# A causal convolution and a routed mixture of experts: a list scheduler with other priorities, and half of the experts' low parts on another engine

## The chip, the core and the metric

One core of a Trainium2 chip runs the kernel. Its engines are TensorE (PE in the profile: matrix products, with PEld for its weight loads), VectorE (DVE), ScalarE (ACT), GpSimd (POOL) and SyncE (SP), each with a queue of its own that is worked off in program order; semaphores order the engines among each other. The metric is the device time of one execution in microseconds.

## The reference

14336 tokens (4 sequences of 3584) of width 192. First a causal convolution with seven taps, whose weights are a softmax for each token and head, then a layer that sends each token to the two best of eight experts:

```python
w = softmax(weight_gen)                       # [B, S, 8 heads, 7 taps]
x = sum over k of w[..., k] * x_pad[s + k]     # causal, 24 columns a head -> N=14336, D=192
logits = x @ w_gate
noisy  = logits + log1p(exp(x @ w_noise)) * noise
top2   = two largest of 8; top2_w = softmax over the two
for e in 8 experts: out[mask] += top2_w * (relu(x[mask] @ w1[e]) @ w2[e])   # w1 192x1024, w2 1024x192
```

## The kernel before

**Chunks.** The tokens go through in 14 chunks of 1024 (8 groups of 128; the first chunk in two halves). For each, `conv` makes the softmax and the seven taps on VectorE: 13 operations on 128x1536 elements (lines 323 and 333, tiles `acc` and `tmp`). `split` writes the result as a float16 high part (ScalarE, line 344) and low part (VectorE, line 348) into a record tile `rec`, of which there are three (RBUF); the high part therefore waits for the scatters of three chunks earlier. `gate` multiplies it with the gate weights on TensorE (line 377, tile `bank`), VectorE adds that up (`lgt`, line 392), `routing` finds the two experts of each token and its place in their queues, with a prefix product on TensorE (lines 500 and 501), and `scatters` sends the records with 16 indirect DMAs of GpSimd (line 407) into the experts' queues `xg` in device memory. `scatter` puts a small memset of a tile `spacer` ahead of each (line 406).

**Rounds.** A round takes 256 rows of each expert's queue: 14 such rounds and one of 128; round c follows chunk c. `prologues` (SP) loads the rows' places and gates (line 794) and the transposed rows `xT` (line 800). Then for each expert four slices: `mm1` (line 856, ten products of 128x256 into a PSUM tile `pm`), `relus` (ScalarE's `hi`, line 871; VectorE's `lo`, line 875), `mm2` (line 896, twelve products of 128x192 into `py`), so 32 slices a round; `finish` multiplies with the gate (ScalarE's `y`, line 908) and adds into `out` with two indirect DMAs of GpSimd for each expert (line 913), a `nop` ahead of each.

**Weights.** They are wanted as float16 high and low parts that together carry a scaled float32 weight. `weights` takes sums of squares (ScalarE, line 678), makes a power of two of them, and writes the high parts (ScalarE). `lows` makes the low parts on TensorE: a float32 product of the weight with a diagonal matrix `dg` (line 715) minus the high part (line 716, `minus` is a negative unit matrix), eight tiles `sums` an expert, each read out by ScalarE (line 719). The parts of the first experts are made ahead of round 0, the others during it.

**What sets the order.** The program is made by a list scheduler, `Sched`. Every stream above is a generator that yields (engine, planned duration, emit, dependencies). The scheduler finds the stream that could start first, and among those on its engine that could start within WAIT of it, takes the one of the highest priority, the second argument of `spawn`. Some priorities are functions: `due` for weights, `hurry` for the routing, which rises when the rounds come near (NEAR, HURRY). GL, AL, ML, UL and XL are planned latencies. The planned times set the order alone; on the chip each engine waits on semaphores, in that order.

Of the kernel before, what the change touches and what calls it, by code (L numbers as in the profile page):

```python
# [41 lines left out]
NEAR = 5  # L42
HURRY = 10
# [6 lines left out]
GL, AL, ML, UL, XL = 5.0, 2.0, 5.0, 15.0, 6.0  # L50


class Sched:
# [90 lines left out]
def moe_kernel(ctx, tc, x_lay, wgen, noise, wgn, w1, w2, xg, out):  # L144
# [131 lines left out]
    def conv(c):  # L276
# [15 lines left out]
        for si in of_chunk[c]:  # L292
# [42 lines left out]
            sch.spawn(split(si, tm["acc"], ta), 12 if c == 0 else 6)  # L335

    def split(si, acc, ta):
# [21 lines left out]
        sch.spawn(gate(si), 12 if c == 0 else 7)  # L359
# [73 lines left out]
    def routing(c):  # L433
# [104 lines left out]
        sch.spawn(scatters(c, pos[0], t), 5)  # L538
        base = fs.tile([P, E], F32, name="begin")
        d = dve(8)  # L540
        for q, (cc, b) in enumerate(ROUNDS):
# [15 lines left out]
            sch.spawn(strays(q, t1), 4)  # L557
# [109 lines left out]
    def due(e):  # L667

        return 10 if e < 2 or e - at[0] < NEAR else 2

    def weights(e):
# [22 lines left out]
        dg = hp.tile([P, 2, P], F32, name="dg", bufs=2)  # L694
        for i in range(2):
            td = yield ("ACT", act(P), lambda: A.activation(dg[:, i], ident, AF.Copy, scale=q[:, 1, i:i + 1]),
                        [t] + before("low", e, 2))
# [3 lines left out]
        ts = yield (None, 0.0, None, [ta])  # L701
        sch.spawn(lows(e, dg, ((wb, u, u2, 0), (wa, t1, t2_, 0), (wc, h2, l2, 1)), td, ts), lambda: due(e))

    def lows(e, dg, parts, td, ts):

        for w, h, l, i in parts:
            n = 512 // w.shape[2]
            n = n if w.shape[1] % n == 0 else 2
            for a in range(0, w.shape[1], n):
# [403 lines left out]
```

## Time and the profile before

| | |
|---|---|
| timed runs, median of 3 | 1298.4 us (1297.04 to 1300.36) |
| the profiled execution, its own time | 1293.18 us |
| its span | 1291.4 us |
| mean granted clock of TensorE, share of full | 0.955 |

The span is what the trace covers; 1.8 us lie around it. The median of the timed runs is 5.2 us above the profiled execution's own time. The rows read from the trace stand below, in groups.

### The profile page before, as it was taken

The page shows a single profiled execution, that of the slowest core. Times are in us where ns is not written, and L with a number is a line of the kernel's source. Part 1 is how long each engine was busy: PE and PEld are TensorE (multiplying, and loading weights), DVE is VectorE, ACT ScalarE, POOL GpSimd, SP SyncE. Part 2 cuts the span into 40 slices and gives each one's busy share as a digit, 9 for nine tenths or more (in the row PEclk, how much of TensorE's full clock was granted, in tenths as well). Part 3 has the DMA queues.
Part 4 walks back from the last instruction along what each step waited for, and adds up shares of the span by engine and source line. Part 5 has one row for each costly group of instructions (what it writes and reads, how often), then busy time and mean ns, then how long its engine had stood idle before and what let it go on. Part 6 is the DMA issues. An engine that isn't in the chain of part 4 may idle for free.

```text
span 1291.4 us, 27931 instructions
## 1 busy us (share of the span) xinstructions
PE 1101.0 (85%) x10958; PEld 975.8 (76%) x10958; DVE 813.7 (63%) x1540; ACT 549.6 (43%) x1231; POOL 731.2 (57%) x781
## 2 busy tenths in 40 slices
PE   0267999999969979889869889969799999999994
PEld 0033677988968969678859879869688889999994
DVE  5447858778868878677858778858644533333331
ACT  6587774444424334324333434323323333333331
POOL 0025165475876847658466574867756777333332
PEclk9998998999999999889989999989898999999997
DMA  9952585537536475455564737546273544334331
GB/s 254 300 164 57 113 203 81 124 75 142 111 58 147 125 98 125 75 104 128 89 126 73 144 65 137 113 60 101 51 102 68 89 82 78 45 50 48 38 39 20
DMA packets 249686, 132.49 MB, mean 103 GB/s; under 512 B 182096, under 2 KB 242000, under 8 KB 247888
## 3 DMA queue, kind: packets, MB, share of 16 engines
q1 hardware_dynamic: 205392, 85.37, 30.3%
q0 software_dynamic: 44160, 45.31, 22.5%
q8 instruction: 86, 1.41, 0.5%
q14 instruction: 48, 0.39, 0.1%
HBM read 38.70 MB, written 58.10 MB: 75 GB/s over the span
## 4 chain that ended last, share of the span: by engine, by line
PE 67%; issue 7%; DMA 7%; ACT 5%; DVE 5%; POOL 4%; SPq 3%; another core or an unknown queue 1%; ACTq 0%; POOLq 0%; DVEq 0%
PE pm L856 34%; PE py L896 29%; POOL xg L407 3%; DMA out<-y,token 2%; PE sums L715 2%; ACT junk L269 2%; DMA xt<-x_lay 2%; SPq L794 1%; POOL out L913 1%; DVE acc L333 1%; DVE tmp L323 1%; DMA xg<-rec,pos 1%; SPq L370 1%; DMA xT<-xg 1%
## 5 line engine op out<-in xcount | busy, mean ns | idle before, releaser
L856 PE MATMUL pm<-xT,wres 128*128 128x256 f16 (+1 forms) x4800 | 601.9, 273 | 27.9 <-DMA xT<-xg 17.9
L913 POOL DMA_INDIRECT out<-y,token x232 | 407.6, 1757 | 364.5 <-ACT y L908 175.2
L896 PE MATMUL py<-wres,hi 128*128 128x192 f16 x3712 | 509.7, 249 | 48.7 <-ACT y L908 18.4
L875 DVE SCALAR_TENSOR_TENSOR lo<-pm,hi 128x512 f16<-128x512 f32 x464 | 316.5, 687 | 345.6 <-ACT hi L871 282.5
L856 PEld LDWEIGHTS <-wres 128*128 128x128 f16 x4800 | 455.5, 99 | 85.6 <-issue 21.5
L871 ACT ACTIVATE hi<-pm 128x512 f16<-128x512 f32 x464 | 275.5, 596 | 568.8 <-PE pm L856 454.4
L896 PE MATMUL py<-wres,lo 128*128 128x192 f16 x1856 | 461.9, 249 | 17.0 <-DVE lo L875 10.5
L896 PEld LDWEIGHTS <-hi 128*128 128x128 f16 x3712 | 343.8, 99 | 71.0 <-issue 39.9
L407 POOL DMA_INDIRECT xg<-rec,pos x224 | 281.3, 1256 | 78.8 <-issue 52.4
L896 PEld LDWEIGHTS <-lo 128*128 128x128 f16 x1856 | 183.7, 99 | 21.1 <-DVE lo L875 13.7
L333 DVE TENSOR_TENSOR acc<-acc,tmp 128x1536 f32<-128x1536 f32 (+1 forms) x90 | 147.9, 1643 | 0.9
L323 DVE TENSOR_TENSOR tmp<-xt,wt 128x1536 f32<-128x1536 f32 (+1 forms) x90 | 147.8, 1643 | 0.7
L908 ACT ACTIVATE y<-py,gate 128x192 f32<-128x192 f32 x232 | 95.5, 418 | 67.0 <-PE py L896 41.5
L406 POOL MEMSET spacer<- 1x1 f32 x224 | 63.5, 283 | 0.1
L715 PE MATMUL sums<-wres,dg 128*128 128x512 f32 (+1 forms) x96 | 53.2, 639 | 7.6 <-ACT wres L719 5.9
L269 ACT ACTIVATE junk<-xt 128x192 f16<-128x192 f32 x118 | 42.7, 362 | 21.9 <-DMA xt<-x_lay 18.6
L529 POOL TENSOR_SCALAR rec<-rr 128x8 f32<-128x8 f32 x14 | 4.5, 319 | 80.4 <-DVE rr L478 79.5
L348 DVE TENSOR_TENSOR rec<-acc,rec 128x512 f16<-128x512 f32 (+2 forms) x30 | 26.8, 898 | 31.8 <-ACT rec L344 31.1
L719 ACT ACTIVATE wres<-sums 128x512 f16<-128x512 f32 (+1 forms) x64 | 34.1, 541 | 25.7 <-PE sums L716 21.2
L715 PEld LDWEIGHTS sums<-wres,dg 128*128 128x128 f32 x96 | 18.2, 215 | 28.2 <-ACT wres L719 17.8
L377 PE MATMUL bank<-wga,xtg 128*128 128x32 f16 x224 | 15.1, 180 | 24.9 <-DMA xtg<-rec 24.5
L598 PE MATMUL sums<-ss,ones 128*128 128x2 f32 x32 | 6.9, 313 | 34.5 <-ACT junk L678 28.0
(132 smaller groups left out, 510.6 us busy)
## 6 DMA issues: line engine op xcount, KB each, us to landing
xt<-x_lay SPq DMA_DIRECT2D x13, 1344.0 KB
out<-zrec SPq DMA_DIRECT2D x14, 768.0 KB
wres<-w SPq DMA_DIRECT2D x6, 768.0 KB
out<-y,token POOLq DMA_INDIRECT x232
xg<-rec,pos POOLq DMA_INDIRECT x224
wt<-wgen SPq DMA_DIRECT2D x14, 224.0 KB
wres<-w SPq DMA_DIRECT2D x6, 512.0 KB
wres<-w SPq DMA_DIRECT2D x12, 256.0 KB
```

The lines of the kernel that those rows point to most:

```text
L269: nc.scalar.activation(q, xtile[s][:, i - first], AF.Square, accum_out=nrm[:, i:i + 1])
L323: V.tensor_mul(tm[key].rearrange("p j (h g) -> p j h g", h=H), xt[:, t:t + n].rearrange("p j (h g) -> p j h g", h=H), w[:, a:a + n].rearra ...
L333: ta = yield ("DVE", cc, lambda: V.tensor_add(tm["acc"], tm["acc"], tm["tmp"]), [])
L406: nc.gpsimd.memset(spacer, 0.0)
L407: i = nc.gpsimd.indirect_dma_start(out=xg, out_offset=bass.IndirectOffsetOnAxis(ap=idx, axis=0), in_=src, in_offset=None)
L715: nc.tensor.matmul(o, dg[:, i], w[:, a:a + n], start=True, stop=False)
L856: nc.tensor.matmul(dst, w[:, c0:c0 + 128], m, start=i == 0, stop=i == 4)
L871: nc.scalar.activation(h[0][:, :n], pm[:, :n], AF.Relu)
L875: T["lo", si] = yield ("DVE", dve(n), lambda: nc.vector.scalar_tensor_tensor(h[1][:, :n], pm[:, :n], 0.0, h[0][:, :n], op0=OP.max, op1=OP. ...
L896: nc.tensor.matmul(dst, h[:, cols], w[:, c0:c0 + D], start=begin, stop=f == F // P - 1 and i == 2, skip_group_check=True)
L908: nc.scalar.activation(y[0], o.py[t // 2][:, (t % 2) * D:(t % 2 + 1) * D], AF.Copy, scale=gate_of[o.c][:, o.e, t:t + 1])
L913: i = nc.gpsimd.indirect_dma_start(out=out, out_offset=bass.IndirectOffsetOnAxis(ap=token[o.c][:, o.e, t:t + 1], axis=0), in_=y[0], in_off ...
```

## The change

All literal priorities become a table PR with other numbers, among them 12.1 where the second chunk's convolution had 3, and 12.3 where `finish` had 7.5. NEAR, HURRY, WAIT and the planned latencies change, and so do two of the planner's durations for GpSimd (1.5 to 1.6, 1.4 to 1.85). Low parts stay on TensorE for experts 0, 4, 5 and 6 (LOWPE); for 1, 2, 3 and 7 they are three `scalar_tensor_tensor` of VectorE, of 1024, 1024 and 1536 elements a partition. The `nop` ahead of each addition becomes a memset of `spacer`, as the scatters have it.

```diff
-NEAR = 5
-HURRY = 10
+NEAR = 2
+HURRY = 12
-GL, AL, ML, UL, XL = 5.0, 2.0, 5.0, 15.0, 6.0
+LOWPE = (0, 4, 5, 6)
+WAIT = 0.29
+PR = dict(split=1.0, gate=8.7, conv1=12.1, conv=4.3, route=7.6, idle=8.7, scatter=1.8, stray=2.1, gates=5.7,
+          finish=12.3, relu=11.4, norms=4.0, rows=9.0, wload=1.0, due=12.1, undue=4.3)
+GL, AL, ML, UL, XL = 3.9, 0.9, 4.4, 17.1, 15.4
...
-            sch.spawn(convs(k + 1), 3)
+            sch.spawn(convs(k + 1), PR["conv1"] if k == 0 else PR["conv"])
...
-                t = yield ("POOL", 1.5, lambda: scatter(c, pos[:, s, i:i + 1], rec[c][:, i, :]), [t0, "zeroed"], 0.37)
+                t = yield ("POOL", 1.6, lambda: scatter(c, pos[:, s, i:i + 1], rec[c][:, i, :]), [t0, "zeroed"], 0.37)
...
+        if e not in LOWPE:
+            sch.spawn(low2(e, lambda: V.scalar_tensor_tensor(
+                l2, wc, q[:, 1, 1:2], h2, op0=OP.mult, op1=OP.subtract), tw), lambda: due(e))
...
+        if e in LOWPE:
+            sch.spawn(lows(e, dg, ((wb, u, u2, 0, 4), (wa, t1, t2_, 0, 4), (wc, h2, l2, 1, 2)), td, ta), lambda: due(e))
+        else:
+            sch.spawn(low1(e, lambda: V.scalar_tensor_tensor(
+                u2, wb, q[:, 1, 0:1], u, op0=OP.mult, op1=OP.subtract), tu,
+                lambda: V.scalar_tensor_tensor(t2_, wa, q[:, 1, 0:1], t1, op0=OP.mult, op1=OP.subtract), ta),
+                lambda: due(e))
+
+    def low1(e, fu, tu, fa, ta):
+        yield ("DVE", dve(F) + 0.06, fu, [tu])
+        T["low1", e] = yield ("DVE", dve(F) + 0.06, fa, [ta])
+
+    def low2(e, fn, t):
+        T["low2", e] = yield ("DVE", dve(8 * D) + 0.06, fn, [t])
...
-                nc.gpsimd.nop()
+                nc.gpsimd.memset(spacer, 0.0)
...
-            ta = yield ("POOL", 1.4, add, [ty + (AL if o.c else 0.0), ("clear", ROUNDS[o.c][0]), ("token", o.c)] + before("added", bi, 1), 0.27)
+            ta = yield ("POOL", 1.85, add, [ty + (AL if o.c else 0.0), ("clear", ROUNDS[o.c][0]), ("token", o.c)] + before("added", bi, 1), 0.27)
...
-                sch.spawn(finish(bj, t), 7.5)
+                sch.spawn(finish(bj, t), PR["finish"])
...
-            sch.spawn(relus(si), 8)
+            sch.spawn(relus(si), PR["relu"])
```

Of the instructions, ScalarE loses 32 read-outs of low parts and eight of the diagonals, TensorE 32 of the 64 tiles, VectorE gains 12 and GpSimd 232 memsets. The lines of the changed kernel lie some 4 to 24 further down than those before.

Where that puts the instructions is shown at three places. **The head, VectorE.** Before, chunk 0's `lgt` and routing follow on chunk 0's low parts (`rec_285`) and the beginning of chunk 1's softmax (`sm`, `wt`):

```order
L348 TENSOR_TENSOR rec_285<-acc,rec_285 128x4x128
L348 TENSOR_TENSOR rec_285<-acc,rec_285 128x4x64
L286 TENSOR_REDUCE sm<-wt 128x64
L287 TENSOR_TENSOR wt<-wt,sm 128x448
L392 TENSOR_REDUCE lgt<-bank 128x64 x2
L450 TENSOR_TENSOR lgt<-lgt,iv 128x128
L456 TENSOR_SCALAR uu<-wide 128x64
```

After, the second half of `lgt` stands behind the thirteenth and last of the 128x1536 operations of chunk 1's convolution:

```order
L327 TENSOR_TENSOR tmp<-xt,wt 128x1536
L337 TENSOR_TENSOR acc<-acc,tmp 128x1536
L396 TENSOR_REDUCE lgt<-bank 128x64
L454 TENSOR_TENSOR lgt<-lgt,iv 128x128
L691 TENSOR_TENSOR iw<-q 128x1 x2
L613 TENSOR_SCALAR q<-q 128x2 x2
L290 TENSOR_REDUCE sm<-wt 128x64
L460 TENSOR_SCALAR uu<-wide 128x64
```

The whole convolution of chunk 1 has moved from behind chunk 0's routing to ahead of it. Two of VectorE's new low parts stand inside that routing and four behind its end.

**Round 0, ScalarE.** Each read-out `wres<-sums` stands for one tile of low parts on TensorE ahead of it. Before, in the middle of round 0:

```order
L719 ACTIVATE wres<-sums 128x4x128 x2
L871 ACTIVATE hi_1110<-pm_1015 128x512
L871 ACTIVATE hi_1116<-pm_1064 128x512
L908 ACTIVATE y_1119<-py,gate 128x192
L719 ACTIVATE wres<-sums 128x2x192
L908 ACTIVATE y_1128<-py,gate 128x192
```

After, from the last read-out of all on:

```order
L743 ACTIVATE wres<-sums 128x2x192
L894 ACTIVATE hi_1144<-pm_1112 128x512
L894 ACTIVATE hi_1181<-pm_1154 128x512
L682 ACTIVATE junk,ss<-wab 128x1024
L931 ACTIVATE y_1206<-py,gate 128x192
L894 ACTIVATE hi_1226<-pm_1187 128x512
```

Of the tiles, 33 stand behind the first slice of round 0 before, and 5 after, the last of them behind its fourth slice.

**Chunks 9 and 12, GpSimd and ScalarE.** Here the numbers of the tiles are kept; chunk 9 and chunk 12 share a record buffer, `rec2`. Before, GpSimd, the last of chunk 9's scatters (`rec2_8714`):

```order
L407 DMA xg<-rec2_8714,pos_10934 131072x196
L913 DMA out<-y4_11463,token_10538 14592x192
L913 DMA out<-y5_11500,token_10538 14592x192
L406 MEMSET spacer_126 1x1
L407 DMA xg<-rec2_8714,pos_10934 131072x196
L913 DMA out<-y0_11590,token_10538 14592x192
```

and ScalarE, where chunk 12's high part (`rec2_11675`) waits for that scatter:

```order
L908 ACTIVATE y0_11590<-py_11468,gate_10537 128x192
L871 ACTIVATE hi3_11608<-pm3_11579 128x512
L908 ACTIVATE y1_11624<-py_11468,gate_10537 128x192
L871 ACTIVATE hi4_11639<-pm4_11611 128x512
L871 ACTIVATE hi2_11671<-pm2_11645 128x512
L344 ACTIVATE rec2_11675<-acc_11153 128x8x192
L871 ACTIVATE hi0_11704<-pm0_11677 128x512
```

After, GpSimd, the last of chunk 9's scatters (`rec2_9070`):

```order
L410 MEMSET spacer_126 1x1
L411 DMA xg<-rec2_9070,pos_10329 131072x196
L935 MEMSET spacer_126 1x1
L936 DMA out<-y4_11142,token_10215 14592x192
L935 MEMSET spacer_126 1x1
L936 DMA out<-y5_11189,token_10215 14592x192
```

and ScalarE, chunk 12's high part (`rec2_12245`):

```order
L894 ACTIVATE hi1_12202<-pm1_12173 128x512
L931 ACTIVATE y3_12211<-py_12037,gate_11368 128x192
L461 ACTIVATE ln_12151<-uu_12150 128x64
L894 ACTIVATE hi2_12239<-pm2_12213 128x512
L348 ACTIVATE rec2_12245<-acc_11719 128x8x192
L894 ACTIVATE hi0_12273<-pm0_12248 128x512
```

Before, the scatter stands behind the addition of `y5_11500`, and the high part that needs its buffer two `y` later on ScalarE. After, it stands ahead of the addition of `y4_11142`, and the high part behind `y3_12211`, eighteen `y` later. The last scatter of chunk c stands ahead of round c's beginning by so many additions, for chunks 1 to 7: before 11, 8, 8, 10, 6, 8, 11; after 6, 6, 6, 8, 8, 8, 10.

## Rows read from the trace of the kernel before

**Rows 1.** The page, part 1: each engine's busy time, its share of the span, and its instructions.

```profile
PE 1101.0 (85%) x10958; PEld 975.8 (76%) x10958; DVE 813.7 (63%) x1540; ACT 549.6 (43%) x1231; POOL 731.2 (57%) x781
```

**Rows 2.** Busy time by stage. Columns: the stage from and to, its length, then busy time and instructions of PE, PEld, DVE, ACT and POOL, TensorE's granted clock as a share of full, the DMA engines' busy share, GB/s. The stages are the head, round 0, rounds 1 to 11 and round 12.

```profile
0.00:123.04 123.04, 48.90 (x150) 23.11 (x151) 74.27 (x155) 87.26 (x211) 26.06 (x58) 0.97 0.73 199
123.04:232.50 109.46, 104.12 (x833) 79.20 (x833) 78.05 (x137) 69.92 (x152) 47.90 (x59) 0.95 0.64 125
232.50:1103.80 871.30, 778.81 (x8035) 711.88 (x8033) 603.77 (x1157) 328.66 (x747) 589.52 (x617) 0.95 0.54 100
1103.80:1170.50 66.70, 66.70 (x708) 63.08 (x706) 23.04 (x40) 25.04 (x49) 25.39 (x19) 1.00 0.39 49
```

**Rows 3.** What TensorE waits for in rounds 1 to 11 (232.5 to 1103.8 us): its line, what ended the wait, us in total, times, the longest.

```profile
PE py L896 <- ACT y L908: 18.4, 4, 11.5
PE py L896 <- ACT hi L871: 18.3, 3, 9.3
PE py L896 <- issue: 18.0, 29, 4.2
PE pm L856 <- DMA xT<-xg: 16.4, 3, 8.4
PE py L896 <- DVE lo L875: 10.5, 7, 4.5
PE pm L856 <- issue: 9.5, 25, 0.9
```

**Rows 4.** The timeline of the head: start, duration, engine, line, instruction, and in brackets the idle time before it and what ended it. VectorE's routing and convolution, GpSimd's first and last scatters with one memset, the first product of round 0.

```profile
69.85 0.29 DVE L392 TENSOR_REDUCE lgt<-bank 128x64 f32<-128x128 f32 x1 [14.48 <-PE bank L377]
86.09 0.17 DVE L536 TENSOR_TENSOR rec<-gg,rec 128x8 f32<-128x8 f32 x1
93.14 1.76 DVE L323 TENSOR_TENSOR acc<-xt,wt 128x1536 f32<-128x1536 f32 x1
...
87.30 1.19 POOL L407 DMA_INDIRECT xg<-rec,pos  x1 [11.19 <-DVE mask L572]
88.50 0.09 POOL L406 MEMSET spacer<- 1x1 f32 x1
88.79 0.97 POOL L407 DMA_INDIRECT xg<-rec,pos  x1 [0.20 <-issue]
90.07 0.97 POOL L407 DMA_INDIRECT xg<-rec,pos  x1 [0.23 <-issue]
99.50 1.49 POOL L407 DMA_INDIRECT xg<-rec,pos  x1 [0.22 <-issue]
112.06 1.49 POOL L407 DMA_INDIRECT xg<-rec,pos  x1 [0.22 <-issue]
...
123.04 0.38 PE L856 MATMUL pm<-xT,wres 128*128 128x256 f16 x2 [1.57 <-DMA xT<-xg]
```

**Rows 5.** The low parts on TensorE: first one tile in the timeline, its two lines; then the busy time of PE and PEld in round 0 of line 715 alone, and of line 716 alone.

```profile
128.19 1.02 PE L715 MATMUL sums<-wres,dg 128*128 128x512 f32 x2
129.05 0.38 PE L716 MATMUL sums<-wres,minus 128*128 128x512 f16 x1
...
123.04:232.50 109.46, 33.98 (x66) 11.62 (x66) 0.95 0.64 125
...
123.04:232.50 109.46, 12.31 (x33) 3.43 (x33) 0.95 0.64 125
```

**Rows 6.** Groups of VectorE instructions by line and shape, over the whole span: busy time, mean ns of one, idle time before them and what ended it. The first has two inputs in SBUF and 1024 elements a partition, the second 1536.

```profile
L348 DVE TENSOR_TENSOR rec<-acc,rec 128x1024 f16<-128x1024 f32 x13 | 15.9, 1222 | 24.9 <-ACT rec L344 24.2 <-issue 0.4 <-POOL spacer L406 0.2
L333 DVE TENSOR_TENSOR acc<-acc,tmp 128x1536 f32<-128x1536 f32 x78 | 136.4, 1749 | 0.5
```

**Rows 7.** Timeline of rounds 9 and 10, ScalarE's records and the product behind each; then the busy times, as in rows 2, of the 4.9 us behind the first.

```profile
860.18 1.48 ACT L344 ACTIVATE rec<-acc 128x1536 f16<-128x1536 f32 x1 [12.90 <-DMA xg<-rec,pos]
862.21 0.50 PE L896 MATMUL py<-wres,hi 128*128 128x192 f16 x2 [9.31 <-ACT hi L871]
931.44 1.48 ACT L344 ACTIVATE rec<-acc 128x1536 f16<-128x1536 f32 x1 [9.92 <-DMA xg<-rec,pos]
933.47 0.50 PE L896 MATMUL py<-wres,hi 128*128 128x192 f16 x2 [7.14 <-ACT hi L871]
...
862.20:867.10 4.90, 4.02 (x22) 3.00 (x23) 4.79 (x12) 2.27 (x6) 2.15 (x2) 0.50 0.62 72
```

**Rows 8.** Timeline, the first products of rounds 3 and 5.

```profile
385.81 1.03 PE L856 MATMUL pm<-xT,wres 128*128 128x256 f16 x4 [8.36 <-DMA xT<-xg]
554.34 0.82 PE L856 MATMUL pm<-xT,wres 128*128 128x256 f16 x3 [6.71 <-DMA xT<-xg]
```

**Rows 9.** Timeline of GpSimd in round 9: an addition, a memset and a scatter, and two additions on end.

```profile
847.94 1.58 POOL L913 DMA_INDIRECT out<-y,token  x1 [0.30 <-issue]
848.92 0.63 POOL L406 MEMSET spacer<- 1x1 f32 x1
849.83 0.98 POOL L407 DMA_INDIRECT xg<-rec,pos  x1 [0.27 <-issue]
853.63 1.60 POOL L913 DMA_INDIRECT out<-y,token  x1 [0.30 <-issue]
855.54 1.55 POOL L913 DMA_INDIRECT out<-y,token  x1 [0.30 <-issue]
```

More of the change, by code (lines that the diff above doesn't have):

```diff
@@ L334, in conv @@
             T["conv", si] = tn
-            sch.spawn(split(si, tm["acc"], ta), 12 if c == 0 else 6)
+            sch.spawn(split(si, tm["acc"], ta), 12 if c == 0 else PR["split"])
     def split(si, acc, ta):
@@ L358, in split @@
         T["loa", si] = yield ("DVE", dve(n * 64), lambda: lows(D, 128, 64), [t])
-        sch.spawn(gate(si), 12 if c == 0 else 7)
+        sch.spawn(gate(si), 12 if c == 0 else PR["gate"])
     def gate(si):
@@ L424, in hurry @@
     def hurry(c):
-        return 7 if upto[c] - at[0] < HURRY else 2.5
+        return PR["route"] if upto[c] - at[0] < HURRY else PR["idle"]
     def route(c):
@@ L537, in routing @@
         T["bend", c] = t
-        sch.spawn(scatters(c, pos[0], t), 5)
+        sch.spawn(scatters(c, pos[0], t), PR["scatter"])
         base = fs.tile([P, E], F32, name="begin")
@@ L556, in routing @@
             T["batch", q] = tb
-            sch.spawn(strays(q, t1), 4)
+            sch.spawn(strays(q, t1), PR["stray"])
     def strays(q, t):
@@ L667, in due @@
     def due(e):
-        return 10 if e < 2 or e - at[0] < NEAR else 2
+        return PR["due"] if e < 2 or e - at[0] < NEAR else PR["undue"]
     def weights(e):
@@ L681, in weights @@
         wc = wc.rearrange("p c d -> p (c d)")
-        for i, x in ((0, wa), (2, wb), (1, wc[:, :4 * D]), (3, wc[:, 4 * D:])):
-            t = yield ("ACT", act(x.shape[1]) + 0.19, lambda: square(i, x), [("wc" if i % 2 else "wab", e)]
+        for i, x, m in ((0, wa, F), (2, wb, F), (1, wc[:, :4 * D], 4 * D), (3, wc[:, 4 * D:], 4 * D)):
+            t = yield ("ACT", act(m) + 0.19, lambda: square(i, x), [("wc" if i % 2 else "wab", e)]
                        + before("scaled", e, 2))
@@ L693, in weights, with diagonal @@
         free = [(k, i) for i in range(e - 1) for k in ("low1", "low2")]
[L694 to L697, printed above, removed]
+        if e in LOWPE:
+            dg = []
+            def diagonal(i):
+                if not i:
+                    dg.append(hp.tile([P, 2, P], F32, name="dg", bufs=2))
+                A.activation(dg[0][:, i], ident, AF.Copy, scale=q[:, 1, i:i + 1])
+            for i in range(2):
+                td = yield ("ACT", act(P), lambda: diagonal(i), [t] + before("dg", LOWPE.index(e), 2))
@@ L704, in lows @@
+    def low1(e, fu, tu, fa, ta):
[3 more added lines that the diff above has]
+        T["low2", e] = yield ("DVE", dve(8 * D) + 0.06, fn, [t])
     def lows(e, dg, parts, td, ts):
[L706 to L709, printed above, removed]
+        for k, (w, h, l, i, n) in enumerate(parts):
+            m = n * (D if i else P)
+            for a in range(0, F // P, n):
@@ L713, in add_up @@
                     box.append(hps.tile([P, 512], F32, name="sums", bufs=2))
-                    o = box[0][:, :n * w.shape[2]]
-                    nc.tensor.matmul(o, dg[:, i], w[:, a:a + n], start=True, stop=False)
+                    o = box[0][:, :m]
+                    nc.tensor.matmul(o, dg[0][:, i], w[:, a:a + n], start=True, stop=False)
                     nc.tensor.matmul(o, minus, h[:, a:a + n], start=False, stop=True)
                 def take():
-                    nc.scalar.activation(l[:, a:a + n], box[0][:, :n * w.shape[2]].rearrange(
+                    nc.scalar.activation(l[:, a:a + n], box[0][:, :m].rearrange(
                         "p (f c) -> p f c", f=n), AF.Copy)
-                k = sums[0]
+                u = sums[0]
                 sums[0] += 1
-                m = n * w.shape[2]
-                t = yield ("PE", 5 * m / 2400 + 0.1, add_up, [td, ts] + before("sum", k, 2))
-                t = T["sum", k] = yield ("ACT", act(m), take, [t])
-            if i or w is parts[1][0]:
+                t = yield ("PE", 5 * m / 2400 + 0.1, add_up, [td, ts] + before("sum", u, 2))
+                t = T["sum", u] = yield ("ACT", act(m), take, [t])
+            if k:
                 T["low2" if i else "low1", e] = t
-        T["low", e] = t
+        T["dg", LOWPE.index(e)] = t
     outz = out[:NTOK].rearrange("(p n) d -> p n d", p=P)
@@ L982, in moe_kernel @@
     sch.spawn(n_loads(), 3)
-    sch.spawn(weight_loads(), 3.5)
-    sch.spawn(norms(), 11)
+    sch.spawn(weight_loads(), PR["wload"])
+    sch.spawn(norms(), PR["norms"])
     sch.spawn(gate_weights(), 13)
@@ L990, in moe_kernel @@
     sch.spawn(clear(), 2)
-    sch.spawn(prologues(), 6)
+    sch.spawn(prologues(), PR["rows"])
     sch.spawn(tensor(), 1)
```

7 lines of the change are left out of this document (3 added, 4 removed).

## The prediction

> **What bounds the kernel now.** I read the busy times first: TensorE works 1101 us of a span of 1291, VectorE 814, GpSimd 731, ScalarE 550 [rows 1]. The table by stage then says where TensorE isn't kept busy [rows 2]. Its first line is the head, up to the first product of round 0: 123.0 us with 48.9 of TensorE work. The second is round 0, 109.5 us. The third is rounds 1 to 11, 871.3 us, or 79.2 each, with 778.8 busy. The fourth is round 12, where TensorE is busy for all of 66.7 us. So 66.7 is the price of a round without a stall, and rounds 1 to 11 lie 871.3 − 11 × 66.7 = 138 above it. A few of the 138 are the gate and prefix products of later chunks, which round 12 no longer has; most of it is stalls and what follows them. The waits of TensorE in that stage [rows 3] have no single owner: 18.4 us for ScalarE's y, 18.3 for its hi, 18.0 and 9.5 of issue, 16.4 for the transposed rows xT, 10.5 for VectorE's lo. A stall costs twice: after the one at 862.2 the granted clock is 0.50, the lower of the two levels, for the 4.9 us that I looked at [rows 7]. So the order of each engine decides, and the order is what is changed.
>
> **The change part by part.** The sum is made against the profiled execution: span 1291.4, its own time 1293.2. The median of the timed runs is 1298.4, or 5.2 more, and I add that at the end.
>
> *The head.* The first product of round 0 waits for the rows that chunk 0's 16 scatters write [rows 4]. Before, VectorE does chunk 0's routing at once: the reduction into lgt at 69.85, after an idle time of 14.48, the last of the records at 86.09, the first scatter at 87.30, the last at 112.06 (ending 113.55), the product at 123.04. After, the 13 large operations of chunk 1's convolution stand ahead of that reduction. They are 13 × 1.75 = 22.8 us [rows 6], and some 3.3 of small softmax operations go with them; the 14.48 of idle time takes in part. So the reduction comes 22.8 + 3.3 − 14.5 = 11.6 late. Six of the new VectorE low parts also stand between there and the first scatter's mask; two of them lie inside the routing itself (1.75 + 1.22 = 3.0). I take 14.7 for both. The scatters then last 26.25 as before, and the last leg 9.5. Term: **+15**. Bounds: +6 if the idle time takes in the small operations too and the scatters, with less beside them, keep the pitch of 1.28 that the first of them have (16 × 1.28 = 20.5); +22 if all six low parts (two of 1.75 and four of 1.22, 8.4) come ahead of it and every scatter takes 1.49.
>
> That scatters beside VectorE are slower is seen in [rows 4]: 0.97 at 88.79, before the convolution starts at 93.14, and 1.49 at 99.50 and 112.06 beside it. The Trainium skill ("SBUF — State Buffer", Who interferes with whom) infers the other thing, that a tensor_tensor does not hold up descriptor generation. By it the scatters of chunk 0 would take 0.97 whatever runs beside them, 16 × 0.52 = 8 us less at most, an estimate. The measurement here differs and decides.
>
> *Round 0.* 32 of the 64 tiles of low parts leave TensorE. Of the tiles still to do once round 0 has begun, 33 stand there before and 5 after, by the order of the two programs: 28 fewer. Price of one: the groups of its two lines cover 33.98 + 12.31 = 46.3 us in round 0 [rows 5], at most 1.40 each, but matmuls overlap in the records; a tile that starts at 128.19 has its second matmul at 129.05, so 0.9 is the floor. Round 0 is 109.5 − 66.7 = 42.8 above a round without stalls, so one tile can't be worth over 42.8/33 = 1.30. I take 1.1, in the middle: 28 × 1.1 = **−31** (bounds −25 and −36). What they become costs VectorE 2 × 1.22 + 1.75 = 4.2 us an expert [rows 6], 16.8 for four; nine of the twelve instructions stand in the head, three in round 0, where VectorE has 109.5 − 78.1 = 31 us idle [rows 2]. ScalarE loses 32 read-outs, which nothing waits for any longer.
>
> *Rounds 1 to 11, ScalarE.* Twice ScalarE stands in its own order at the operation that writes the records of a chunk (rec) and waits 12.90 and 9.92 us for scatters that read the same buffer three chunks earlier; the hi behind it is late, and TensorE waits 9.31 and 7.14 [rows 7]. Before, chunk 12's rec stands two y later than the addition behind which chunk 9's last scatters stand; after, it stands 18 y later, and chunk 13's likewise. Both waits should go: 16.5, and the 4.9 and 5.4 us behind them at half the clock give back about half, 5.1. Term: **−21.5**; the bound is 0, if another instruction becomes the late one.
>
> *Rounds 1 to 11, xT.* Round 5 begins 6.71 and round 3 begins 8.36 late, for rows just scattered [rows 8]. Chunk 5's last scatter stood 6 additions ahead of the round's end, after it 8; its prefix product stands 6 slices earlier too. So the 6.71, and 2.8 for the clock behind it, go: −9.5. Chunks 2 and 3 move the other way, from 8 additions ahead to 6. At 1.9 an addition [rows 9] each may come 3.8 later, 7.6 in all; half of it is taken, since chunk 5's pitch is no rule for the others: +3.8. Chunk 1's scatters stand between more additions than before (11 ahead to 6): +3. Term: **−2.7**, bounds −20 and +11.
>
> *Rounds 1 to 11, the rest.* Issue and y [rows 3] are 46 us for which I see no reason in the order either way. The convolutions stretch from 27.4 to 29.8 slices a chunk, which thins VectorE's load; I take 0, bounds −20 and +12.
>
> *Memsets at additions.* Scatters have had one ahead of them all along: 0.97 each at a pitch of 1.27. An addition, with a nop ahead, takes 1.55, and addition follows addition at 855.54 − 853.63 = 1.91 [rows 9]. Behind the addition of 847.94 the memset starts 0.98 later and ends with it, so that the scatter starts 1.89 behind the addition. No row has a memset ahead of an addition. Nearest for no gain: 1.89 against 1.91, the tail of 0.57 stays with the addition even where a memset follows. Nearest for a gain: the same indirect DMA as a scatter has no such tail, 0.57 × 16 = 9.1 us of GpSimd a round. For a loss: the memset's 0.63, seen there, plus 0.27 of issue, 0.9. I take 0, since the two pitches agree and the memset can run ahead of what the addition waits for.
>
> The sum: 1293.2 + 15 − 31 − 21.5 − 2.7 = 1253.0, and with 5.2, **1258**.
>
> **The rivals.**
> *The memset shortens additions.* GpSimd is busy 589.5 of 871.3 in rounds 1 to 11 and runs without a pause through each chunk's scatters, so up to 9.1 a round could come off; over 11 rounds a quarter to a third of that, about 27: 1258 − 27 = 1231. For it: scatters beside memsets have no tail. Against it: 1.89 and 1.91. The order may also remove stalls of the kind that I set at 0, with a like result. Together 0.25.
>
> *The waits come back.* Rounds 1 to 11 stay at 871, because a list order freed at one place waits at the next (five kinds of wait of 10 to 18 us each stand there now [rows 3]). Then only head and round 0 count: 1293.2 + 15 − 31 + 5.2 = 1282. Chance 0.15.
>
> *The memset lengthens additions: slower.* At 0.9 each GpSimd has 14.4 us more a round, of the 79.2 − 53.6 = 25.6 that it has free. With a third of it on the path, 4.8 × 11 = 53: 1311. It decides from the point where it eats the 40 us of the sum, 40/11/16 × 3 = 0.68 us an addition. Against it: the memset waits for nothing but the memset ahead of it, and takes 0.09 between scatters, which keep their pitch with one each [rows 4]. Chance 0.08.
>
> **How the numbers follow.** My forecast, 1258, has 0.45, with a range of its own of 1238 to 1277. The gain rival has 0.25, the returning waits 0.15, the slower one 0.08; 0.07 is left for mixtures, 0.02 of it faster, 0.03 about level and 0.02 slower. What a measurement of this kernel tells from no change is about 0.3%, or 4 us: faster is below 1294.5, slower above 1302.3. The returning waits end at 1282, but 0.03 of them come close enough to count as the same. Faster 0.45 + 0.25 + 0.12 + 0.02 = 0.84, same 0.06, slower 0.10. The range leaves out the slower cases and the farthest of the gain: 1212 to 1292.
>
> **What would show it.** Right: the first product of round 0 at 131 to 145 us; round 0 near 78; no wait of ScalarE over 5 us at a rec in rounds 9 to 11; round 5 starting without a wait; additions at a pitch near 1.9. Wrong: the mean of an addition at 1.0 to 1.2 us instead of 1.76 (the gain rival); a memset of 0.6 ahead of each addition and a pitch of 2.5 (the slower one); rounds 1 to 11 still near 79 each, with TensorE's waits under other names (the waits that come back); a head past 145 us.

## The result and the profile after

The changed kernel takes 1208.0 us (median of 4; 1205.5 to 1214.4) beside 1297.7 of the kernel before: ratio 0.933, 95% interval 0.930 to 0.936. The changed kernel ran twice more beside the kernel before, with 0.945 (0.942 to 0.949) and 0.940 (0.935 to 0.945); the chips differ, so ratios to the kernel before on the same chip are compared below. The forecast was 1258 with a range of 1212 to 1292: the direction was right, the size too small, the result just below the range. One profile among those below, that of a_al14 (AL at 1.4), is of an execution 1.6% above the fastest of its kernel.

The profiled execution took 1206.6 us, its span 1204.7. Busy times, for [rows 1]:

```profile
PE 1051.8 (87%) x10862; PEld 953.8 (79%) x10862; DVE 825.7 (69%) x1552; ACT 526.0 (44%) x1191; POOL 749.8 (62%) x1013
```

The stages of [rows 2]: head, round 0, rounds 1 to 11, round 12, and the last part, whose length was 54.3 before.

```profile
0.00:140.40 140.40, 48.64 (x161) 23.37 (x162) 113.24 (x194) 99.68 (x235) 25.63 (x55) 0.74 0.75 198
140.40:217.60 77.20, 70.57 (x726) 64.02 (x726) 58.15 (x121) 37.80 (x87) 51.63 (x73) 0.98 0.60 123
217.60:1021.80 804.20, 763.60 (x8033) 704.81 (x8034) 596.08 (x1144) 324.54 (x747) 600.41 (x791) 0.98 0.59 109
1021.80:1088.40 66.60, 66.60 (x707) 62.98 (x705) 23.58 (x41) 25.41 (x49) 29.84 (x41) 1.00 0.39 53
...
1155.00:1204.70 49.70, 35.83 (x538) 35.60 (x536) 12.25 (x21) 13.65 (x26) 16.11 (x21) 0.89 0.30 29
```

So the head grew by 17.4, round 0 lost 32.3, rounds 1 to 11 lost 67.1, the last part 4.6: together −86.6. The 17.4 leans on one execution of the kernel before: b_mem, below, has the order of before and a head of 128.5, and the changed kernel's heads were 139.8 to 141.2. What TensorE waits for in rounds 1 to 11, for [rows 3]:

```profile
PE pm L879 <- DMA xT<-xg: 21.1, 4, 8.8
PE pm L879 <- issue: 6.2, 21, 0.4
PE py L919 <- issue: 5.5, 16, 0.5
PE py L919 <- ACT hi L894: 4.0, 1, 4.0
...
PE py L919 <- ACT y L931: 2.4, 1, 2.4
PE py L919 <- DVE lo L898: 1.3, 4, 0.7
```

Most of the waits for y (18.4 before), hi (18.3), lo (10.5) and issue (27.5) are gone. Those for xT are not: of the 21.1, 6.2 end with the first product of round 1 and so lie in round 0, which leaves 14.9 in the stage beside 16.4 before. Fewer stalls are also less time at the lower of the two clocks: the granted clock of the stage rose from 0.95 to 0.98, and TensorE's busy time fell from 778.8 to 763.6 for as many matmuls. So of the 67.1, 15 are the same work done in less time, and 52 are idle time that is gone (92.5 before, 40.6 after).

### The profile page after: what moved, and what is told of

It reads as the page before. It is cut to its first block, busy times and chain, and to the rows that moved or that the text cites. A ratio compares the mean times of both kernels' runs of the same rounds, so it can differ in the third digit from the quotient of the medians.

```text
span 1204.7 us, 27979 instructions
## 1 busy us (share of the span) xinstructions
PE 1051.8 (87%) x10862; PEld 953.8 (79%) x10862; DVE 825.7 (69%) x1552; ACT 526.0 (44%) x1191; POOL 749.8 (62%) x1013
## 3 DMA queue, kind: packets, MB, share of 16 engines
q1 hardware_dynamic: 205392, 85.37, 32.3%
q8 instruction: 85, 1.39, 0.5%
## 4 chain that ended last, share of the span: by engine, by line
PE 52%; POOL 15%; DMA 10%; DVE 7%; issue 6%; ACT 6%; SPq 4%; another core or an unknown queue 0%; POOLq 0%; DVEq 0%; ACTq 0%
PE pm L879 27%; PE py L919 24%; POOL xg L411 8%; POOL out L936 7%; DMA xt<-x_lay 3%; DMA out<-y,token 3%; SPq L817 2%; DVE acc L337 2%; DVE tmp L327 2%; DVE lo L898 2%; DMA xg<-rec,pos 1%; DMA xT<-xg 1%; DMA wres<-w 1%; ACT junk L682 1%; ACT junk L273 1%
## 5 line engine op out<-in xcount | busy, mean ns | idle before, releaser
L879 PE MATMUL pm<-xT,wres 128*128 128x256 f16 (+1 forms) x4800 | 594.3, 271 | 30.2 <-DMA xT<-xg 23.4
L919 PE MATMUL py<-wres,hi 128*128 128x192 f16 x3712 | 503.3, 247 | 9.8 <-ACT hi L894 4.0
L411 POOL DMA_INDIRECT xg<-rec,pos x224 | 292.0, 1304 | 76.4 <-issue 67.5
L935 POOL MEMSET spacer<- 1x1 f32 x232 | 102.8, 443 | 0.1
L410 POOL MEMSET spacer<- 1x1 f32 x224 | 53.3, 238 | 0.1
L602 PEld LDWEIGHTS sums<-ss,ones 128*128 128x128 f32 x32 | 7.1, 282 | 43.0 <-ACT junk L682 43.0
L739 PE MATMUL sums<-wres,dg 128*128 128x512 f32 (+1 forms) x48 | 29.3, 698 | 5.3 <-ACT wres L743 3.1
L739 PEld LDWEIGHTS sums<-wres,dg 128*128 128x128 f32 x48 | 9.9, 230 | 22.3 <-ACT wres L743 10.4
```

Of the source, the lines that this page charges most:

```text
L410: nc.gpsimd.memset(spacer, 0.0)
L411: i = nc.gpsimd.indirect_dma_start(out=xg, out_offset=bass.IndirectOffsetOnAxis(ap=idx, axis=0), in_=src, in_offset=None)
L879: nc.tensor.matmul(dst, w[:, c0:c0 + 128], m, start=i == 0, stop=i == 4)
L919: nc.tensor.matmul(dst, h[:, cols], w[:, c0:c0 + D], start=begin, stop=f == F // P - 1 and i == 2, skip_group_check=True)
L935: nc.gpsimd.memset(spacer, 0.0)
```

## Experiments

Each runs beside the kernel before on the same chip. "Rounds" is rounds 1 to 11 of its profiled execution, and "lag" the number of hi of later slices that stand ahead of a block's second y in ScalarE's order, on the mean of these rounds. Times are in us.

| kernel | ratio, 95% interval | head | round 0 | rounds | waits for y | lag |
|---|---|---|---|---|---|---|
| before | 1 | 123.0 | 109.5 | 871.3 | 18.4 | 4.4 |
| changed | 0.933 (0.930 to 0.936) | 140.4 | 77.2 | 804.2 | 2.4 | 3.5 |
| a_same, the changed kernel again | 0.945 (0.942 to 0.949) | 139.8 | 74.9 | 806.4 | 3.6 | 3.5 |
| a_same2, and again | 0.940 (0.935 to 0.945) | 141.2 | 77.1 | 815.6 | 3.5 | 3.5 |
| b_mem | 1.001 (0.998 to 1.005) | 128.5 | 109.9 | 864.5 | 19.5 | 4.4 |
| b_low | 0.990 (0.985 to 0.994) | 126.0 | 96.8 | 867.8 | 5.7 | 4.5 |
| b_pr | 0.989 (0.986 to 0.992) | 136.4 | 109.2 | 849.7 | 12.1 | 4.4 |
| b_poollat | 0.974 (0.971 to 0.978) | 128.8 | 106.1 | 837.5 | 0 | 3.1 |
| b_pool | 1.025 (1.020 to 1.030) | 127.4 | 112.5 | 891.1 | 87.1 | 6.0 |
| b_poolal | 0.988 (0.984 to 0.992) | 129.6 | 111.6 | 847.3 | 13.5 | 3.8 |
| a_poollat | 0.965 (0.960 to 0.970) | 138.3 | 80.1 | 845.3 | 26.7 | 5.4 |
| a_low | 0.944 (0.939 to 0.950) | 126.8 | 110.3 | 788.0 | 2.6 | 3.5 |
| a_conv1_9 | 0.941 (0.936 to 0.946) | 133.2 | 90.5 | 796.0 | 0 | 3.2 |
| a_l0123 | 0.957 (0.953 to 0.961) | 127.8 | 117.1 | 802.0 | 0.3 | 3.4 |
| a_al2 | 0.989 (0.984 to 0.994) | 144.9 | 76.9 | 855.2 | 69.1 | 5.8 |
| a_al14 | 0.945 (0.938 to 0.952) | 143.0 | 78.5 | 822.0 | 31.1 | 5.8 |
| a_al04 | 0.937 (0.931 to 0.943) | 140.9 | 78.6 | 803.1 | 0 | 2.6 |
| a_wait3 | 0.940 (0.936 to 0.945) | 141.3 | 76.7 | 797.9 | 4.5 | 3.5 |
| a_fin | 0.961 (0.957 to 0.966) | 144.1 | 79.0 | 839.2 | 5.6 | 3.9 |
| a_l0123_n11 | 0.932 (0.927 to 0.936) | 136.5 | 75.8 | 801.7 | 0 | 3.2 |

One order repeats to some 12 us: the changed kernel's rounds were 804, 806 and 816 in three profiled executions. Its ratio was 0.933, then 0.945 (a_same, expected at 0.933) and 0.940, so kernels whose ratios lie within 0.933 to 0.945 aren't told from it here.

### The memset

```diff
-                nc.gpsimd.nop()
+                nc.gpsimd.memset(spacer, 0.0)
```

> The kernel before, with a memset of spacer in place of the nop ahead of each addition and nothing else; the order of all other instructions is that of before. If the memset costs nothing (the step of the prediction): the same time within 0.3%, 1294 to 1302, additions still 1.76 us on the mean, two on end at a pitch of 1.9. If it shortens additions: mean near 1.2 and 20 to 30 us less, about 1270. If it lengthens them: over 1310.

Measured: 1.001, 1296.4 us. Its groups of additions and of the memsets ahead of them:

```profile
L936 POOL DMA_INDIRECT out<-y,token x232 | 408.9, 1762 | 353.8 <-ACT y L931 178.0 <-DMA out<-y,token 53.8 <-ACT hi L894 42.3
L935 POOL MEMSET spacer<- 1x1 f32 x232 | 85.2, 367 | 0.3
```

An addition still takes 1.76 us. Two on end in the changed kernel, for [rows 9]:

```profile
770.24 1.63 POOL L936 DMA_INDIRECT out<-y,token  x1 [0.23 <-issue]
771.24 0.67 POOL L935 MEMSET spacer<- 1x1 f32 x1
772.17 1.58 POOL L936 DMA_INDIRECT out<-y,token  x1 [0.27 <-issue]
```

The memset lies in the addition's tail and ends with it; the pitch is 1.93, where it was 1.91. The tail is the addition's own.

### Half of the low parts, or the priorities, alone

b_low is the kernel before with

```diff
+LOWPE = (0, 4, 5, 6)
...
+        if e not in LOWPE:
+            sch.spawn(low2(e, lambda: V.scalar_tensor_tensor(
...
```

> The kernel before, with the low parts of experts 1, 2, 3 and 7 on VectorE and all priorities and planned numbers as before. The term of the prediction: round 0 shorter by 25 to 36 us, rounds 1 to 11 within 10 us of 871, so about 1267. If the low parts also free rounds 1 to 11 (the part that the forecast missed): rounds 1 to 11 near 830 and the time near 1230. If they only move stalls: over 1285.

Round 0 fell by 12.7 only and not by 25 to 36, rounds 1 to 11 stayed at 868 in all, and round 1 grew from 74.7 to 94.6. In this order 16 of the 32 tiles that are left still stand in round 0. Round 2 begins at 317.4, with TensorE waiting 13.4 us for chunk 2's rows and 6.2 for their routing before. I read this as the tiles having been cover: without them TensorE waits for the chunks, which VectorE makes. In all 1% was gained.

b_pr has the change's table of priorities, NEAR, HURRY and WAIT, and nothing else of it.

> The kernel before, with the table of priorities, NEAR, HURRY and WAIT of the change alone; planner's durations and latencies, low parts and nop as before. Theory priorities (finish and relu ahead of all side work keep TensorE supplied): rounds 1 to 11 fall by 40 us or more; with the longer head (+17) and round 0 unchanged about 1260. Theory planner: rounds 1 to 11 within 15 us of 871, and with the longer head 1300 to 1320.

Neither expectation was met: rounds fell by 21.6, of which up to 12 is the spread between executions, and head and round 0 together are 13 longer. One thing b_pr does show: none of its records waits for a scatter any more, while ScalarE still waits 31.9 us for scatters at that line in b_low and 14.6 in b_poollat. So it is the priorities that take these waits away.

### The planner's numbers alone

```diff
-GL, AL, ML, UL, XL = 5.0, 2.0, 5.0, 15.0, 6.0
+GL, AL, ML, UL, XL = 3.9, 0.9, 4.4, 17.1, 15.4
...
-                t = yield ("POOL", 1.5, lambda: scatter(
+                t = yield ("POOL", 1.6, lambda: scatter(
...
-            ta = yield ("POOL", 1.4, add,
+            ta = yield ("POOL", 1.85, add,
```

> The kernel before, with the planner's numbers alone: durations of a scatter 1.6 and an addition 1.85, and GL, AL, ML, UL, XL of the change; priorities, low parts and nop as before. Theory planner (the plan charged 1.4 for an addition that takes 1.9, so that scatters and additions stood ahead of where GpSimd really was and ScalarE waited for y buffers): rounds 1 to 11 fall by 40 us or more, from 871 to under 831, with TensorE's waits for ScalarE's y below 5 us; time near 1255. Theory priorities: rounds 1 to 11 within 15 us of 871, time 1285 to 1310.

Of the change's parts this gains most by itself: 2.6%, rounds down by 34, a little under the 40 expected. TensorE's waits there:

```profile
PE py L919 <- DVE lo L898: 17.0, 13, 4.5
PE py L919 <- ACT hi L894: 16.1, 8, 3.5
PE pm L879 <- DMA xT<-xg: 14.9, 3, 10.7
PE pm L879 <- issue: 8.9, 22, 1.0
PE py L919 <- issue: 5.3, 16, 0.9
```

No wait for y is left. a_poollat takes the same numbers out of the changed kernel:

> The changed kernel with the planner's old durations (1.5 for a scatter, 1.4 for an addition) and old GL, AL, ML, UL, XL; its priorities, its low parts and the memsets kept. Theory planner: the waits for ScalarE's y (18 us before, none with the planner's numbers alone) come back, rounds 1 to 11 lengthen by 30 us or more from 804, time near 1240. Theory priorities: under 15 us lost, below 1225.

```profile
PE py L918 <- ACT y L930: 26.7, 13, 6.3
```

Rounds grow by 41 and the waits for y are back. So the numbers count in either company. Which of them? b_pool has only the two durations:

```diff
-                t = yield ("POOL", 1.5, lambda: scatter(
+                t = yield ("POOL", 1.6, lambda: scatter(
...
-            ta = yield ("POOL", 1.4, add,
+            ta = yield ("POOL", 1.85, add,
```

> The kernel before with the two planned durations of GpSimd alone (1.6 and 1.85); latencies, priorities, low parts and nop as before. If these two numbers carry what the planner's numbers gave together (rounds 1 to 11 from 871 to 838): rounds 1 to 11 near 840, waits for y gone, time near 1262. If the latencies carry it: rounds 1 to 11 near 865 and y waits of 10 us or more, time near 1290.

Neither: it is 2.5% slower, and TensorE waits for y 40 times.

```profile
PE py L919 <- ACT y L931: 87.1, 40, 10.6
```

The durations need a partner. b_poolal adds AL alone, and a_al2 puts only AL back in the changed kernel:

```diff
-GL, AL, ML, UL, XL = 3.9, 0.9, 4.4, 17.1, 15.4
+GL, AL, ML, UL, XL = 3.9, 2.0, 4.4, 17.1, 15.4
```

> The kernel before with the planned durations of GpSimd (1.6 and 1.85) and AL 0.9, all other latencies, priorities and low parts as before. If AL is the partner of the durations: as with all the planner's numbers, rounds 1 to 11 near 838, hardly a wait for y, ratio near 0.974. If not: waits for y as with the durations alone (87 us), ratio above 1.01.

> The changed kernel with one number put back: AL 2.0 in place of 0.9, the planned time between a y and its addition. If AL decides whether the plan fits GpSimd (the longer durations alone gave 87 us of waits for y): waits for y return to 20 us or more, rounds 1 to 11 from 804 to 835 or more, time 1235 to 1260. If the other latencies do it: rounds 1 to 11 within 12 us of 804.

b_poolal: waits for y fall from 87 to 13.5 and the ratio from 1.025 to 0.988; that is nearly three quarters of the way to 0.974, so AL is the main partner, not the only one. a_al2: one number costs 51 us of rounds and brings 69 us of waits for y.

```profile
PE py L918 <- ACT y L930: 69.1, 41, 6.8
```

Between the two, and beyond, with AL 1.4 and 0.4:

> The changed kernel with AL 1.4, half way between the changed 0.9 and the old 2.0. If waits for y grow with AL once the plan holds GpSimd for fuller than it is: between the two (rounds 1 to 11 at 804 and 855, waits for y 2 and 69 us): rounds 1 to 11 near 825, y 20 to 40, ratio near 0.96. If 0.9 is a lucky order among many: anything from 800 to 860, without relation to the y waits.

> The changed kernel with AL 0.4, about what lies between a y and its addition where GpSimd is idle (0.28 in the trace). If the plan only has to be no slower than the chip: rounds 1 to 11 within 12 us of 804, no waits for y. If a plan too early makes ScalarE stand for y buffers: waits for ScalarE's hi or y of 15 us or more, rounds 1 to 11 over 820.

```profile
PE py L918 <- ACT y L930: 31.1, 21, 5.9
...
PE pm L878 <- DMA xT<-xg: 23.0, 4, 8.4
PE py L918 <- issue: 6.7, 14, 1.7
PE py L918 <- ACT junk L272: 4.0, 1, 4.0
```

The first row is of AL 1.4, the other three are the longest waits with AL 0.4. The waits for y are 0, 2, 31 and 69 us at 0.4, 0.9, 1.4 and 2.0. (The 822 and the 31 of AL 1.4 are read with care, and its ratio can't be told from that of the changed kernel in the two later comparisons.) A plan that is early by half a microsecond costs nothing.

How AL does it can be read from the orders, in the column "lag". With AL 2.0 and the longer durations a block's second y stands behind some six later hi; with AL 0.9 behind 3.5. That y empties the py tile which TensorE needs two blocks, or eight slices, on. On the whole the waits for y go with the lag: 6.0 and 5.8 have 87 and 69 us, 5.4 has 27, 4.4 has 18, 3.1 and 2.6 none; with AL 1.4 the lag is 5.8 and the waits 31. There are exceptions: b_low has 5.7 us at 4.5, and b_poolal 13.5 at 3.8.

Why the plan places the second y so late stands in its code. The stream `finish` offers a block's second y only once the block's first addition has its place. That addition waits, in the plan, for the additions of the block ahead (`before("added", bi, 1)`), and each addition waits for AL after its y. So AL and the planned duration of an addition stand in a chain that runs from block to block, and when this chain is planned longer than TensorE's work on a block, the second y falls behind. The other reading, that the plan thinks the y tiles come free late, doesn't fit: the first y of a block takes such a tile too, and it stands behind 1.9 to 2.4 later hi in every kernel of the table. The chain is read from the code; that AL moves the lag, and that lag and waits go together, is shown.

### Luck, and the priority of TensorE's suppliers

A list order with other numbers is another order. a_wait3 changes a number that stands for nothing on the chip, a_fin the priorities of finish and relu:

```diff
-WAIT = 0.29
+WAIT = 0.3
```

> The changed kernel with WAIT 0.30 in place of 0.29, a number without a meaning for any engine: how far a mere reshuffling moves the time. If orders with the same planned numbers are worth about the same: rounds 1 to 11 within 12 us of 804, ratio 0.93 to 0.95. If the gain is mostly the luck of one order: 15 us or more lost.

```diff
-          finish=12.3, relu=11.4, ...
+          finish=7.5, relu=8, ...
```

> The changed kernel with the old priorities of finish (7.5) and relu (8) alone, below those of the routing's idle level and the gates' 8.7, in place of 12.3 and 11.4. If the priority of TensorE's suppliers is what the table gave (the table alone took 15 to 22 us from rounds 1 to 11): rounds 1 to 11 at 820 to 830, with waits for hi and y of 15 us or more. If not: within 12 us of 804.

a_wait3 is another order, and the changed kernel within what can be told (a_al04 likewise): the gain does not hang on one lucky order. a_fin loses 35 us of rounds in its profiled execution, which is 10 us above its median, but not by the waits expected:

```profile
PE bank L503 <- DVE th L495: 23.8, 5, 8.4
PE pm L878 <- DMA xT<-xg: 18.3, 3, 8.7
PE py L918 <- DVE lo L897: 6.3, 4, 3.7
```

TensorE stands in its own order at the prefix product and waits for VectorE's routing, which the changed kernel hardly shows (0.4 to 2.1 in its three profiled executions). Why the lower priority leads there was not looked into.

### The head, round 0 and the choice of experts

a_low leaves all low parts on TensorE, a_conv1_9 lowers the priority of chunk 1's convolution, a_l0123 moves experts 4 to 7 rather than 1, 2, 3 and 7; all else as changed.

```diff
-LOWPE = (0, 4, 5, 6)
+LOWPE = (0, 1, 2, 3, 4, 5, 6, 7)      a_low
+LOWPE = (0, 1, 2, 3)                  a_l0123
...
-PR = dict(split=1.0, gate=8.7, conv1=12.1, ...
+PR = dict(split=1.0, gate=8.7, conv1=9, ...     a_conv1_9
```

> The changed kernel with the low parts of all eight experts on TensorE; priorities, planner's numbers and memsets kept. By the prediction's term for round 0: 25 to 36 us slower, all of it in round 0 (77 to 105), near 1238. If moving the low parts gains little by itself, as the kernel before with that edit alone suggests (14 us, round 0 shorter and round 1 longer): 10 to 18 us slower, near 1222.

> The changed kernel with priority 9 in place of 12.1 for the second chunk's convolution; all else kept, the plan made anew. Chunk 0's routing then stands behind 7 of the 13 large operations of that convolution, with the others between its steps. If the order of VectorE sets the head: the first product of round 0 some 8 to 10 us earlier than 140, and the time near 1200 unless chunk 1's rows are late for round 1. If chunk 1 is what round 1 then waits for: round 1 longer by as much, and no gain.

> The changed kernel with the low parts of experts 0 to 3 on TensorE and of 4 to 7 on VectorE, in place of 0, 4, 5, 6 and 1, 2, 3, 7. In its order all 32 tiles stand ahead of round 0, none in it, and chunk 0's routing again stands ahead of chunk 1's convolution with no low part of VectorE before it. If the longer head comes from VectorE's low parts of early experts and not from the priority of the convolution: first product of round 0 near 127 as with all low parts on TensorE (before 123, changed 140), round 0 near 78 as changed, rounds 1 to 11 at 790 to 810, so 10 us or more below the changed kernel, near 1195. If the priority makes the head: near 138, and the time as changed.

> The changed kernel once more, beside the one above on the same chip, for the comparison between the two. 0.933 of the kernel before, as first measured.

In time, a_low isn't told from the changed kernel (0.944): round 1 begins 19.5 us later, and rounds 1 to 11 take 16 less. So this change isn't shown to gain anything by moving half of the low parts, and neither of the two slower times expected came true. a_low has a head of 126.8 although the convolution's priority is 12.1: in its order chunk 0's routing stands ahead of that convolution again. So in the changed kernel the convolution comes first through the priority and the moved low parts together: the priority alone doesn't do it (a_low, b_pr), the moved low parts alone don't either (b_low). a_conv1_9 has a head 7 shorter and a round 0 that is 13 longer, and the time of the changed kernel. a_l0123 has the head that was expected (127.8) and no tile in round 0, and yet round 0 takes 117. Its waits of TensorE from the head's end to the start of round 1:

```profile
PE pm L878 <- DMA xT<-xg: 26.6, 1, 26.6
PE bank L380 <- DMA xtg<-rec: 22.6, 8, 12.7
PE py L918 <- DVE lo L897: 1.7, 1, 1.7
```

(The 26.6 ends with the head.) TensorE is done with round 0 and stands at chunk 1's gate; round 1 begins at 244.9, at the end of a further wait:

```profile
244.91 0.61 PE L878 MATMUL pm<-xT,wres 128*128 128x256 f16 x2 [19.69 <-DMA xT<-xg]
```

So head and round 0 are not two terms but one: the start of round 1 is the later of TensorE's work and chunk 1's rows. It lies at 232.5 before, where TensorE comes to it without a wait; at 217.6 changed, 223.7 in a_conv1_9, 237.1 in a_low and 244.9 in a_l0123 it waits for the rows, from 6 to 20 us. The early convolution that lengthens the head buys the earlier rows. If so, a_l0123 gains with the convolution ahead. That takes the old priority of the norms, on which its softmax weights rest:

```diff
-          ... norms=4.0, ...
+          ... norms=11, ...
```

> The changed kernel with the low parts of experts 0 to 3 on TensorE and of 4 to 7 on VectorE (as in a_l0123), and in addition priority 11 in place of 4.0 for the norms. In its order chunk 1's convolution again stands ahead of chunk 0's routing, all 32 tiles stand ahead of round 0, and VectorE has no low part in the head. If chunk 1's rows are what ends round 0: the first product of round 0 between 128 and 138 (no low parts in VectorE's way), round 1 beginning at 203 to 213 (changed 217.6, a_l0123 244.9), rounds 1 to 11 at 790 to 815, and the time 5 to 15 us below the changed kernel's. If VectorE's four experts' low parts within round 0 (16.8 us) now delay chunk 1: round 1 at 217 or later and no gain.

> The changed kernel once more beside the one above on the same chip, for the comparison: 0.933 to 0.945 of the kernel before.

Round 1 begins at 212.3, within the 203 to 213 expected, and the kernel takes 1204.9 us beside 1218.1 of the changed one: ratios of 0.932 (0.927 to 0.936) and 0.940 (0.935 to 0.945), 0.9% faster than the changed kernel by the ratios (the intervals just overlap, but each of its six times lies below each of the six beside it) and 7% than the one before. But the gain isn't where it was looked for. Chunk 2's rows are late instead:

```profile
308.65 0.59 PE L878 MATMUL pm<-xT,wres 128*128 128x256 f16 x2 [16.93 <-DMA xT<-xg]
```

Round 3 begins at 376.6, in the changed kernel beside it at 374.1; what it gains lies in rounds 3 to 11, 637 us against 660. The changed kernel had 648 and 652 there in its other two profiled executions, and the 637 come from the fastest of six executions, so part of that is the spread of one order, and the rest has no cause that these runs tell apart.

## Why the prediction was wrong, by its steps

Of the 50 us between the forecast and the result, 43 lie in rounds 1 to 11, which were to lose 24 and lost 67. The rest is the last part (4.6) and the median, which lies 1.4 above the profiled execution and not 5.2; the misses of head and round 0 nearly cancel.

**Head, +15: right.** It grew by 17.4, and the row on which it rests moved the way that was worked out: the reduction into lgt came at 86.36, 16.5 later than before (in b_mem, with the order of before, it stands at 74.94).

```profile
86.36 0.28 DVE L396 TENSOR_REDUCE lgt<-bank 128x64 f32<-128x128 f32 x1
94.84 1.82 DVE L710 SCALAR_TENSOR_TENSOR wres<-wres,q 128x1536 f16<-128x1536 f32 x1
96.66 1.28 DVE L717 SCALAR_TENSOR_TENSOR wres<-wres,q 128x1024 f16<-128x1024 f32 x1
104.28 1.19 POOL L411 DMA_INDIRECT xg<-rec,pos  x1 [11.17 <-issue]
129.10 1.48 POOL L411 DMA_INDIRECT xg<-rec,pos  x1 [0.23 <-issue]
```

The 11.6 that I gave it was up to 5 too small; the low parts took 1.8 and 1.3, near the 1.75 and 1.22 taken for them, but the scatter came about as long after the reduction as before (17.9 now, 17.5 then), so they cost 0.5 and not 3.0: VectorE was idle for 7.3 of the 17.5 before. The scatters kept 26.3 against 26.2.

**Round 0, −31: the size was right (−32.3), the working was not.** I priced tiles on TensorE. a_l0123 has none left in round 0 and takes 117 us. Taking tiles away brings the start of round 1 forward only as far as chunk 1's rows come, and it is the early convolution that brings these forward: TensorE still waits 6.23 at the start of round 1. b_low, with the low parts alone, gained 13 in round 0 and gave it back in round 1.

**ScalarE's records, −21.5: right by its rows.** In the changed kernel no record waits for a scatter, and TensorE's waits for hi fell from 18.3 to 4.0; ScalarE's idle time before line 348 is 13.2 us in all, each time for VectorE.

```profile
  DVE acc L337: 13.2, 7
```

**xT, −2.7: wrong by some 7, and read from too little.** The waits went from 16.4 to 21.1. Round 5's fell from 6.71 to 0.68. Rounds 1 and 2 wait 6.23 and 8.82, where I had given 3 and half of 3.8, and round 3 still 5.38.

```profile
217.59 0.61 PE L879 MATMUL pm<-xT,wres 128*128 128x256 f16 x2 [6.23 <-DMA xT<-xg]
298.90 0.61 PE L879 MATMUL pm<-xT,wres 128*128 128x256 f16 x2 [8.82 <-DMA xT<-xg]
373.87 0.60 PE L879 MATMUL pm<-xT,wres 128*128 128x256 f16 x2 [5.38 <-DMA xT<-xg]
512.88 0.50 PE L879 MATMUL pm<-xT,wres 128*128 128x256 f16 x3 [0.68 <-DMA xT<-xg]
```

But such a wait isn't fixed by the order. In a_same and a_same2, the same kernel, round 5 waits 5.06 and 4.30, so the sign "round 5 starting without a wait" came true in the first execution alone; and in b_mem, with the order of before, round 3 waits 1.14 where [rows 8] has 8.36. Round 5 of a_same, and round 3 of b_mem:

```profile
510.25 0.40 PE L879 MATMUL pm<-xT,wres 128*128 128x256 f16 x1 [5.06 <-DMA xT<-xg]
...
388.03 0.39 PE L879 MATMUL pm<-xT,wres 128*128 128x256 f16 x2 [1.14 <-DMA xT<-xg]
```

**The rest of rounds 1 to 11, 0: the step that failed.** I wrote that I saw no reason in the order for the 46 us of issue and y, and bounded it at −20. Those waits and lo's fell by 41 (issue from 27.5 to 11.7, y from 18.4 to 2.4, lo from 10.5 to 1.3), and part of the 15 us by which TensorE's work got shorter stands behind them. A reason stood in the diff: AL from 2.0 to 0.9, which I had not priced at all, together with the durations. Taken out of the changed kernel, all the planner's numbers cost 41 us of the 67 (a_poollat); AL alone costs 51 (a_al2, ratio 0.989 beside 0.965), more than all of them, since the longer durations then stand without it. Taking out the priorities of finish and relu costs 35 (a_fin). These don't add up, since each is taken from the whole; alone the planner's numbers give 34, the priorities 22 and the low parts 4, each give or take the 12 us of one order's spread. The share of y is AL's by these runs; which edit took the waits of issue and lo away they don't single out. The place to read it was ScalarE's order: how many hi stand ahead of each second y.

**Memset, 0: right** (b_mem, 1.001), and with it the rival that shortens additions and the one that lengthens them both fall. The gain rival's other half, that the order removes stalls of the kind set at 0, is what happened; its time of 1231 was still 23 too long. The rival by which the waits come back falls too: those for xT grew, but by 5 us. **The last part**, for which I had no term, lost 4.6 us; it is 54 again in a_al2 (1210.2 to 1264.3).

## What to carry to other kernels

A list scheduler's planned durations and latencies are part of the kernel: correct one kind alone and the order can get worse (1.025), with its partner better (0.988), and with all of them better still (0.974), so those that stand in one planned chain are set against the trace together. When an order changes, look first at what stands ahead of each instruction that frees a buffer, not only at the waits that the old profile names. A stage that is covered by two chains is one term, the later of the two: taking work from one engine there gains nothing past the other's. And a wait seen once is compared with a second execution of the same order before it becomes a term: those at the start of a round moved by 4 to 7 us between executions.

## What the runs showed of the hardware that was not expected

A memset behind an indirect accumulating DMA doesn't shorten it; it starts about 1.0 us after the addition and ends with it (0.67 at 771.24), while one behind a scatter takes 0.09 (at 105.48, behind the scatter of 104.28). Scatters are slower beside the convolution in the changed kernel as in [rows 4] (1.48 at 129.10, beside that of chunk 2). Beside the new low parts, whose inputs both lie in SBUF, it is mixed. Low parts start at 105.79 (1.81 long), 108.05 and 109.31 (1.26 and 1.28): the first scatter below runs wholly beside one and takes 0.98, the next two run partly or wholly beside them and take 1.39 and 1.42, and the last has mostly small operations beside it. What tells the first from the next two was not looked into.

```profile
105.77 0.98 POOL L411 DMA_INDIRECT xg<-rec,pos  x1 [0.20 <-issue]
107.06 1.39 POOL L411 DMA_INDIRECT xg<-rec,pos  x1 [0.21 <-issue]
108.75 1.42 POOL L411 DMA_INDIRECT xg<-rec,pos  x1 [0.21 <-issue]
110.47 0.97 POOL L411 DMA_INDIRECT xg<-rec,pos  x1 [0.22 <-issue]
```
